# The second chunk of a fused attention and SwiGLU kernel: two orderings of the same work, and where float64 weights get their sign bits

## The chip, the cores and the metric

The kernel runs on one core of a Trainium2 chip. The metric is the device time of one execution in microseconds (us); lower is better. TensorE (PE) does the matmuls and PE transposes, VectorE (DVE) and ScalarE (ACT) the elementwise work, GpSimd (POOL) here only memsets and DMA issues, SyncE (SP) only DMA issues.

## The reference, cut to what matters

```
B, H, S, D = 4, 8, 768, 48;  d_model = H*D = 384;  d_ff = 1536
f = sigmoid(f_logit)                              # B,H,S,D
for t in range(S):                                # per batch and head
    state = f[:, :, t, :, None] * state + outer(k[:, :, t], v[:, :, t])
    y[:, :, t] = q[:, :, t] @ state
x   = y.transpose(0, 2, 1, 3).reshape(B * S, H * D)      # 3072 x 384
out = (silu(x @ w_gate) * (x @ w_val)) @ w_out           # weights arrive as float64
```

## The kernel before

**Units and chunks.** The sequence is cut into 6 chunks of 128 positions. A unit is one batch in one chunk; unit u is batch u % 4 of chunk u // 4. Each unit runs `attention(u)`, a generator that stops at some 15 places so that its steps can be set between other work. For a unit the kernel forms running products of the gates on DVE (two scans), multiplies k and q by them, takes the scores on PE (`sc`, L700), masks them on DVE (`A`, L719), multiplies by v on PE (`y`), and carries a state of 48x48 per head (`decayed`, `dS`, `state`). A chunk's four units make 512 tokens, which then go through the feed-forward part.

**Stages.** Stage 1 is the attention of chunk 0. Stage 2 is the feed-forward of chunk 0 by plain matmuls, with the attention of chunk 1 (units 4 to 7) set between them, and beside it the conversion of all weights. Stage 3 is the feed-forward of chunks 1 to 5 by products over sums of blocks (15 products in place of 18, 7 in place of 8), with the attention of the chunks after set between them. The change is in stage 2.

**Two ways to turn f, k and q.** A unit needs f, k and q with the head dimension on partitions. Plain units load rows and turn them by PE transposes against an identity (`fTp`, `kTp`, `qTp`, L614; 4 matmuls each), and turn k back the same way (`kt`, L704). Units for which `by_squares(u)` holds load the data already laid out in squares and turn them by DVE's 32x32 transposes (L630, L641, L685); k goes back through a DVE transpose (L668) and two DMAs over DRAM. In stage 2 of the kernel before units 5, 6 and 7 go by squares.

**Weights.** The float64 weights come in 18 pieces of 768 KB: six pairs of `w_gate` and `w_val`, two hidden blocks each, and six pieces of `w_out`. `fetch` issues the DMA on SP's queue into one of four buffers `w64`. `sizes` has ACT write the low mantissa part (`up`, L491) and the magnitude (`top`, L495). `join` has DVE clamp (L505), shift (L508 or L512) and add (L510, L516). The sign is the open matter: pieces listed in `SIGNED` (9 of the 18) get it from a third ACT instruction (L494); the others from a third DVE instruction that takes the two top bits out of `w64` (L514). `up` and `top` have two buffers each. The first pair is handled in halves, so that there are 20 joins.

**Feed-forward of chunk 0.** `mlp_plain(0)` gives 12 gate products and 12 val products (L836), each followed by a Silu on ACT or a multiplication on DVE, and 12 down steps (L859), each of four matmuls of 128x384, one for each of the four batches. PSUM has four banks for these (`m`) and four for attention (`a`).

**Sums of weights.** `weight_sums` gives 32 DVE additions over `w_both` into `extra` and back into `w_both`, which stage 3 needs; `token_sums` gives further ones over `xT`.

**Order of stage 2.** Each step of `mlp_plain` carries a planned duration (`PLAIN`, `PLAIN_DOWN`). Lists name the planned time at which each further step is issued: `JOINS_AT`, `SIZES_AT`, `FETCHES_AT`, `EARLY` for the four units and `SUMS_AT`. `in_turn_of_time` merges them:

```
for took, f in steps:
    come_in()                 # issue all that is due by now
    before = lagging[:]; lagging.clear()
    f()
    for g in before: g()      # Silu or multiplication, one step late
    now += took
```

After it `in_order` chains all of stage 2's instructions of PE, DVE, ACT and SP in that order.

Of the kernel before, what the change touches and what calls it, by code (L numbers as in the profile page):

```python
# [290 lines left out]
def short_path(ctx, tc, ident, least, judge, q, k, v, f_logit, moe_w_gate, moe_w_val, moe_w_out, out):  # L291
# [80 lines left out]
    middle = const.tile([128, 1], FP32, tag="middle", name="middle")  # L372
    nc.gpsimd.memset(middle, 32767.5)
# [29 lines left out]
    def by_squares(u):  # L403
        return u >= SQUARES * B - 3
# [26 lines left out]
    by_pool = []  # L431

# [26 lines left out]
    def weight_piece(dst, src, parts, signs):  # L459
# [27 lines left out]
        def sizes(m):  # L487
            lo, hi = halves(m)
            up = wst.tile(shape, I32, tag="up", name="up", bufs=NPART)
            ends = up.bitcast(U16).rearrange("p b a (n two) -> p b a n two", two=2)  # L490
            nc.scalar.activation(ends[:, :, :, :, 0], lo.bitcast(U32), AF.Copy, scale=2.0 ** -29)  # L491
            top = wst.tile(shape, I32, tag="top", name="top", bufs=NPART)
            if signs:
                nc.scalar.activation(ends.bitcast(mybir.dt.float16)[:, :, :, :, 1], high_ends(m), AF.Sign, bias=middle, scale=-1.0)  # L494
            nc.scalar.activation(top.bitcast(FP32), hi.bitcast(FP32), AF.Abs, scale=2.0 if signs else 1.0)  # L495
            kept["up", m], kept["top", m] = up, top

        def join(m, what=("clamp", "add")):
            lo, hi = halves(m)
            up, top = kept["up", m], kept["top", m]  # L500
            if "add" in what and "clamp" not in what:
                nc.vector.tensor_tensor(dst[:, part(m)].bitcast(I32), top, up, ALU.add)
                return
            step = 0x800000 if signs else 0
            nc.vector.tensor_scalar(top.bitcast(FP32), top.bitcast(FP32), as_float(0x38000000 + step), as_float(0x47F00000 + step),  # L505
                                    op0=ALU.max, op1=ALU.min)
            if signs:
                nc.vector.tensor_single_scalar(top, top, 3, op=ALU.logical_shift_left)  # L508
                if "add" in what:
                    nc.vector.tensor_tensor(dst[:, part(m)].bitcast(I32), top, up, ALU.add)  # L510
                return
            nc.vector.tensor_scalar(top, top, 3, 0x3FFFFFFF, op0=ALU.logical_shift_left, op1=ALU.bitwise_and)  # L512
            ends = up.bitcast(U16).rearrange("p b a (n two) -> p b a n two", two=2)
            nc.vector.tensor_single_scalar(ends[:, :, :, :, 1], high_ends(m), 0xC000, op=ALU.bitwise_and)  # L514
            if "add" in what:
                nc.vector.tensor_tensor(dst[:, part(m)].bitcast(I32), top, up, ALU.add)  # L516
# [15 lines left out]
    SIGNED = (4, 6, 7, 8, 9, 11, 15, 16, 17)  # L532

    def add_piece(dst, src, parts=1):
        fetch, *rest = weight_piece(dst, src, parts, len(fetches) in SIGNED)
        fetches.append(fetch)
        for group, fs in zip((sizes, joins), rest):
            group += fs
# [32 lines left out]
    owner = {}  # L571

    def owned(u, *names):
        assert all(owner[nm] == u for nm in names), (u, owner)

    def attention(u):
        b, c = units[u]
        rot = u % NROT if c < SQUARES else 0
# [16 lines left out]
        def decay():  # L595
            nonlocal diagonal
            if c:
                owner["decayed"] = u
                nc.vector.tensor_tensor(decayed[:, :, 0:D], states[b], whole.broadcast_to((128, HP, D)), ALU.mult)
# [28 lines left out]
        owner["gate", rot] = u  # L628
# [18 lines left out]
        owner["tail", rot] = owner["start"] = u  # L647
        owned(u, ("gate", rot))
# [12 lines left out]
        owned(u, ("tail", rot))  # L661
# [14 lines left out]
        if in_squares:  # L676

            (nc.scalar.copy if c >= SQUARES else nc.vector.tensor_copy)(least[:, u, :], whole.rearrange("p a t -> p (a t)"))
            whole = least[:, u, :].unsqueeze(2)
        owned(u, ("gate", rot), ("tail", rot), "start")  # L680
# [7 lines left out]
        owned(u, ("gate", rot), ("tail", rot))  # L688
        multiply(qT, qp, pairs(gate)[:, :, 1:N1])
        nc.gpsimd.memset(pairs(gate)[:, :, 0:1], 0.0)  # L690
# [37 lines left out]
        if c:  # L728
            owned(u, "decayed")
# [63 lines left out]
        if c == 0:  # L793
            nc.scalar.copy(states[b], dS)
        elif c < NCH - 1:
            owned(u, "decayed")
            nc.vector.tensor_tensor(states[b], decayed[:, :, 0:D], dS, ALU.add)
        yield

    def load_after(u, what):  # L800

        if u + 1 < len(units) and u + 1 != SQUARES * B:
            load(u + 1, what)

# [25 lines left out]
    def mlp_plain(c):  # L830
# [13 lines left out]
        def gate(j):  # L844
            p = product(w_gate, j, "gate")
            lag(nc.scalar.activation, part(j), p, AF.Silu)

        def val(j):
            p = product(w_val, j, "val")
            lag(nc.vector.tensor_tensor, part(j), part(j), p, ALU.mult)  # L850

        return [*[(PLAIN, lambda j=j, f=f: f(j)) for f, j in ((gate, 0), (val, 0), (gate, 1), (val, 1))],
                *[(PLAIN, lambda j=j, f=f: f(j)) for i in range(2, NF, 2) for f in (gate, val) for j in (i, i + 1)],
                *[(PLAIN_DOWN, f) for f in downs_abreast(c, h)]]
# [13 lines left out]
    def downs_abreast(c, h):  # L868
# [3 lines left out]
        def step(n):  # L872
# [3 lines left out]
            for b in range(B):  # L876
                down_part(banks[b], c, h, b, n)
                if n == NF - 1:
                    ob = rooms_of[b // 2][:, b % 2, :]
                    (nc.vector.tensor_copy if b % 2 else nc.scalar.copy)(ob, banks[b])  # L880
                    nc.gpsimd.dma_start(out=out[b * S + c * C:b * S + (c + 1) * C, :], in_=ob)
# [13 lines left out]
    PRODUCT, DOWN, PLAIN, PLAIN_DOWN = 0.86, 3.9, 2.57, 2.65  # L895
# [7 lines left out]
    def chain(k, q, qmul, turn=None, head=None):  # L903
# [10 lines left out]
        (chain(2.6, 4, 8.6), chain(14.5, 20, 23), chain(30, 37, 43.2), chain(57.4, 57.8, 61)),  # L914
# [12 lines left out]
    def score_bank(u):  # L927
# [6 lines left out]
    JOINS_AT = (0.8, 4.5, 5, 7.6, 13.2, 16.3, 20.3, 27.2, 29.6, 36.1, 38.7, 43.3, 46.6, 47.8, 55.3, 55.4, 67.6, 70.8)  # L934
    SIZES_AT = (0.39, 2.4, 6.2, 11.1, 13.2, 18.4, 18.6, 22.1, 31.8, 38, 39.8, 40.1, 43.1, 50.8, 53, 56, 64.8)
    FETCHES_AT = (-1.1, 0.6, 5.5, 5.9, 6, 9.2, 10.6, 21.1, 23.6, 27, 35.5, 35.5, 37.8, 42.4)
    EARLY = (
        (-1.01, 4.17, 4.58, 9.7, 9.87, 10.5, 11, 11.5, 12, 13.4, 17.3, 22, 28.4, 28.41, 33),
        (26, 31.3, 32.8, 34.3, 34.6, 34.6, 36.1, 37.4, 38.2, 40.6, 43.3, 43.4, 50.8, 54.81, 56),
        (46.2, 49.2, 50.7, 51.4, 51.5, 57, 57.6, 58, 62, 63.9, 64.4, 65.5, 68.2, 68.21, 70),  # L940
        (63, 64, 66.8, 66.9, 67.4, 67.9, 68.6, 71.6, 73.3, 75.9, 76, 76.7, 78, 78.41, 80.3))
    SUMS_AT = (64.3, 64.5, 72.58, 72.7, 74.06, 74.74, 75.3, 75.42, 75.98, 76.02, 76.18, 76.3, 76.66, 76.86,
        77.34, 77.54, 78.22, 78.5, 79.18, 79.86, 81.22, 81.26, 81.26, 81.34, 81.62, 81.9, 81.94, 82.58, 82.58, 82.7,
        83.2)
    LATE_SUMS_AT = (23,)
# [57 lines left out]
    def lag(f, *args):  # L1003
        lagging.append(lambda: f(*args))  # L1004
# [217 lines left out]
    def in_turn_of_time(waiting, steps):  # L1222

        waiting.sort(key=lambda x: x[0])
        now = 0.0

        def come_in():
            while waiting and waiting[0][0] <= now:
                waiting.pop(0)[1]()

        come_in()
        for took, f in steps:
            come_in()
            before = lagging[:]
            lagging.clear()
            f()
            for g in before:
                g()
            now += took
        come_in()  # L1240
        for g in lagging:
            g()
        lagging.clear()
        assert not waiting
# [41 lines left out]
    first_join(("clamp"))  # L1286
    sizes.pop(0)()
    run(B - 1, 3)
    first_join(("add"))
# [5 lines left out]

    waiting = [(t, sizes.pop(0)) for t in SIZES_AT]
    waiting += [(t, joins.pop(0)) for t in JOINS_AT]
    waiting += [(t, fetches.pop(0)) for t in FETCHES_AT]
    assert not fetches and not sizes and not joins
    waiting.append((-0.02, lambda: sigmoid_ahead(B)))  # L1300
    for b, at in enumerate(EARLY):
        run_of = attention(B + b)
        waiting += [(t, lambda run_of=run_of: next(run_of)) for t in at]
    sums_of = [weight_sums(odd) for odd in range(2)]
    sums = sums_of[0][0:7] + sums_of[1][0:7] + sums_of[0][7:] + sums_of[1][7:]
    waiting += zip(SUMS_AT, sums[:len(SUMS_AT)])
    in_turn_of_time(waiting, mlp_plain(0))
    in_order(mark, (mybir.EngineType.PE, mybir.EngineType.DVE, mybir.EngineType.Activation, mybir.EngineType.SP))

# [20 lines left out]

    assert len(SUMS_AT) + len(LATE_SUMS_AT) == len(sums)
    waiting += zip(LATE_SUMS_AT, sums[len(SUMS_AT):])
    waiting += [(at, f) for at, f in zip(DOWN_SUMS_AT, down_weight_sums())]
    blocks = {}

    def blocks_of(c):
        yield from blocks[c]
# [8 lines left out]
    in_turn_of_time(waiting, (step for c in range(1, NCH) for step in blocks_of(c)))  # L1346
# [78 lines left out]
```

## Time and profile before

| | |
|---|---|
| median of 3 runs | 597.66 us (597.51 to 597.72) |
| the profiled execution | 597.51 us, of which span 595.8 us and 1.71 us around it |
| stage 1, stage 2, stage 3 in the profile | 0 to about 30, 30 to 138.4, 138.4 to 595.8 us |
| PE, DVE, ACT, POOL busy over the span | 585.5, 479.3, 301.1, 112.8 us |
| granted TensorE clock | 1.000 |

Times are in us from the start of the span. In lists of instructions in order of time the first column is the start, the second the duration; where an engine waited, brackets give how long and for whom. Instructions of one engine overlap slightly, so that the distance from start to start is often a little under the duration. A matmul's end is modelled, so that a busy PE is not a PE at its peak.

### The profile page before, as it was taken

Reading aid. Unit: us, or ns where it says so; the run is one execution under the profiler, and the core shown is the slowest. Engines: PE = TensorE matmul, PEld = TensorE weight load, DVE = VectorE, ACT = ScalarE, POOL = GpSimd, SP = SyncE. Lnnn points to the kernel's source line nnn. Section 1 sums busy time; section 2 is a strip of 40 time slices with the busy share of each in tenths; the row PEclk is TensorE's granted clock in tenths of the full one; section 3 lists DMA queues with packets and bytes.
Section 4 is the critical chain, followed back from the end, with each engine's and each line's share of the span. In section 5 each row is a group of like instructions: output and inputs, shape, how many; then the busy total and the mean of one; then the engine's idle time right before and its main releaser. Section 6 shows DMA issues by size and latency. Waiting matters only on the chain.

```text
span 595.8 us, 10874 instructions
## 1 busy us (share of the span) xinstructions
PE 585.5 (98%) x3972; PEld 481.8 (81%) x3972; DVE 479.3 (80%) x830; ACT 301.1 (51%) x563; POOL 112.8 (19%) x240
## 2 busy tenths in 40 slices
PE   7899999999999999999999999999999999999996
PEld 4744444667888999888999888899988899988896
DVE  7997998999989877998986888994978972666741
ACT  3488677025877322676640667632476730356600
POOL 3140345202132330212030030330030330000000
PEclk9999999999999999999999999999999999999999
DMA  9999487233666565542345332543231100100001
GB/s 205 253 307 286 142 217 186 60 98 107 122 117 110 96 150 136 138 100 64 84 117 137 99 80 62 112 111 99 74 99 28 29 10 6 53 2 1 2 1 56
DMA packets 106291, 61.86 MB, mean 104 GB/s; under 512 B 64200, under 2 KB 97032, under 8 KB 106232
## 3 DMA queue, kind: packets, MB, share of 16 engines
q1 hardware_dynamic: 93800, 45.96, 31.0%
q0 software_dynamic: 10992, 13.19, 10.0%
q10 hardware_dynamic: 1440, 1.97, 0.9%
q8 instruction: 32, 0.52, 0.4%
q14 instruction: 27, 0.22, 0.1%
HBM read 47.64 MB, written 8.13 MB: 94 GB/s over the span
## 4 chain that ended last, share of the span: by engine, by line
PE 98%; DVE 1%; ACT 0%; issue 0%; DVEq 0%
PE o L1151 20%; PE A L1052 18%; PE B L1052 15%; PE c L1052 6%; PE o L1052 6%; PE o L859 5%; PE gate L836 5%; PE val L836 5%; PE sc L700 4%; PE o L1214 3%; PE y L746 3%; PE y L767 2%; PE dS L787 2%; PE y L742 2%; PE kt L704 1%; PE fTp L614 0%
## 5 line engine op out<-in xcount | busy, mean ns | idle before, releaser
L757 POOL DMA_DIRECT2D xT<-yT x120 | 59.8, 506 | 53.4 <-ACT yT L750 49.0
L1052 PE MATMUL A<-xs,w_both 128*128 128x256 f32 x240 | 62.2, 382 | 0.0
L1151 PE MATMUL o<-w_out,h 128*128 128x192 f32 x360 | 62.0, 327 | 0.0
L1151 PEld LDWEIGHTS o<-w_out,h 128*128 128x128 f32 x360 | 58.7, 190 | 1.0 <-issue 0.2
L1057 ACT COPY c<-A 128x512 f32<-128x512 f32 x40 | 23.3, 583 | 60.5 <-PE A L1052 59.4
L1057 ACT COPY aside<-A 128x512 f32<-128x512 f32 x60 | 35.2, 586 | 32.9 <-PE A L1052 32.7
L951 DVE TENSOR_TENSOR c<-c,aside 128x512 f32<-128x512 f32 x60 | 41.1, 685 | 12.8 <-ACT aside L1057 11.1
L1052 PEld LDWEIGHTS A<-xs,w_both 128*128 128x128 f32 x240 | 44.9, 190 | 6.6
L1004 DVE TENSOR_TENSOR h<-h,c 128x256 f32<-128x256 f32 x100 | 40.6, 414 | 7.6 <-ACT h L1068 7.3
L954 DVE TENSOR_TENSOR c<-c,aside 128x512 f32<-128x512 f32 x60 | 41.0, 684 | 2.7 <-ACT aside L1057 2.7
L1068 ACT ACTIVATE h<-c 128x256 f32<-128x256 f32 x100 | 39.4, 417 | 5.0 <-DVE c L951 3.8
L719 DVE TENSOR_TENSOR A<-sc,causal 128x512 f32<-128x512 f32 x48 | 30.9, 685 | 13.4 <-PE sc L700 13.4
L1151 PE MATMUL o<-ws,h 128*128 128x192 f32 x240 | 41.5, 328 | 0.0
L1052 PE MATMUL B<-xs,w_both 128*128 128x256 f32 x160 | 41.3, 380 | 0.0
L1052 PE MATMUL A<-xs,extra 128*128 128x256 f32 x160 | 41.2, 380 | 0.0
L1052 PE MATMUL c<-xT,w_both 128*128 128x256 f32 x160 | 41.1, 379 | 0.0
L1052 PE MATMUL B<-xT,extra 128*128 128x256 f32 x160 | 41.0, 379 | 0.0
L1057 ACT COPY aside<-B 128x512 f32<-128x512 f32 x60 | 35.2, 586 | 9.0 <-PE B L1052 7.0
L1151 PEld LDWEIGHTS o<-ws,h 128*128 128x128 f32 x240 | 39.1, 190 | 0.5
L954 DVE TENSOR_TENSOR c<-o,c 128x512 f32<-128x512 f32 x40 | 27.4, 686 | 11.0 <-ACT h L1068 6.2
L951 DVE TENSOR_TENSOR c<-c,o 128x384 f32<-128x384 f32 x15 | 8.2, 548 | 34.8 <-PE o L1151 34.8
L690 POOL MEMSET gates<- 128x4 f32 x24 | 3.6, 150 | 169.0 <-DVE qT L593 163.9
(163 smaller groups left out, 1240.2 us busy)
## 6 DMA issues: line engine op xcount, KB each, us to landing
fsquares<-in_f_logit_dram SPq DMA_DIRECT2D x64, 96.0 KB, 4.1
qsquares<-in_q_dram SPq DMA_DIRECT2D x64, 96.0 KB, 2.3
ksquares<-in_k_dram SPq DMA_DIRECT2D x64, 96.0 KB, 2.4
w<-in_moe_w_gate_dram SPq DMA_DIRECT2D x6, 768.0 KB
w<-in_moe_w_val_dram SPq DMA_DIRECT2D x6, 768.0 KB, 6.5
w<-in_moe_w_out_dram SPq DMA_DIRECT2D x6, 768.0 KB, 8.8
v<-in_v_dram SPq DMA_DIRECT2D x19, 192.0 KB, 2.8
turn<-ksquares SPq DMA_DIRECT2D x40, 64.0 KB, 2.2
```

The lines of the kernel that those rows point to most:

```text
L700: nc.tensor.matmul(sc[par][:, a * C:(a + 1) * C], lhsT=kT[r, a, :], rhs=qT[r, a, :], start=True, stop=True)
L719: nc.vector.tensor_tensor(A[:, par], sc[par].rearrange("p (a t) -> p a t", t=C), causal.unsqueeze(1).broadcast_to((128, HP, C)), ALU.mult)
L757: (nc.gpsimd if c >= SQUARES else nc.sync).dma_start(out=xT[c][f % 128:f % 128 + n, f // 128, b * C:(b + 1) * C], in_=yT[r:r + n, par, a / ...
L836: nc.tensor.matmul(p, lhsT=w[:, j, i, :], rhs=xT[c][:, i, :], start=(i == 0), stop=(i == KT - 1))
L859: nc.tensor.matmul(p, lhsT=hidden_tile(h, n // 2)[:, n % 2 * 2 + b // 2, b % 2 * C:(b % 2 + 1) * C], rhs=w_out[:, j, :], start=(n == 0), s ...
L951: nc.vector.tensor_tensor(dst, a, b, ALU.add)
L954: nc.vector.tensor_tensor(dst, a, b, ALU.subtract)
L1004: lagging.append(lambda: f(*args))
L1052: nc.tensor.matmul(p[name][:, n, :], lhsT=weights_of[a][:, n, j, :], rhs=tokens[b], start=fresh and n == 0, stop=True, skip_group_check=True)
L1057: nc.scalar.copy(t, p[name])
L1068: nc.scalar.activation(dst, src[:, 0, :], AF.Silu)
L1151: nc.tensor.matmul(p[:, n, :], lhsT=lhsTs[j][:, n * C:(n + 1) * C], rhs=rhs[:, j, :], start=first and j == order[0] and n == 0, stop=j == ...
```

## The change

The changed kernel orders stage 2 in another way, and three pieces of work go to other engines with it.

1. The lists of times are gone. The first steps of stage 2 are written out one by one and chained by `in_order`; the rest is made by `take_turns`, which hands out the steps of units 4 to 7 evenly among the feed-forward steps, with one `weights()` (one fetch, one size, one join) after each pair of products and four more among the down steps, and the sums woven into the down steps. This rest is not chained: the scheduler of the language places it.
2. `SIGNED` is gone: all 18 pieces get their sign on DVE. ACT's third instruction goes away nine times; DVE's third one comes nine times.
3. `by_squares` starts at unit 6 in place of unit 5: unit 5 loads rows through SP's queue and is turned on PE.
4. The Silu and the multiplication follow their product at once and no longer lag a step; the four output DMAs of chunk 0 go from GpSimd's queue to ACT's; the copy of `least` for units 6 and 7 goes from DVE to ACT; all 32 sums lie ahead of stage 3's lists (one had been in stage 3).

Stage 1 and the order of PE in stage 3 are as before.

```
-        return u >= SQUARES * B - 3
+        return u >= SQUARES * B - 2
...
-            if signs:
-                nc.scalar.activation(ends...[:, :, :, :, 1], high_ends(m), AF.Sign, bias=middle, scale=-1.0)
-            nc.scalar.activation(top.bitcast(FP32), hi.bitcast(FP32), AF.Abs, scale=2.0 if signs else 1.0)
+            nc.scalar.activation(top.bitcast(FP32), hi.bitcast(FP32), AF.Abs)
...
-    SIGNED = (4, 6, 7, 8, 9, 11, 15, 16, 17)
...
-                    nc.gpsimd.dma_start(out=out[b * S + c * C:b * S + (c + 1) * C, :], in_=ob)
+                    nc.scalar.dma_start(out=out[b * S + c * C:b * S + (c + 1) * C, :], in_=ob)
...
+    def attention_steps(c):
+        runs = [attention(c * B + b) for b in range(B)]
+        order = sorted((2 * b + s, b, n) for b in range(B)
+                       for s, n in enumerate((1, 8, 3, 3) if by_squares(c * B + b) else (3, 6, 3, 3)))
+        return [lambda b=b, n=n: [next(runs[b]) for _ in range(n)] for _, b, n in order]
...
+    def take_turns(first, second, rest):
+        done = 0
+        n = len(first) - rest
+        for i, f in enumerate(first):
+            f()
+            want = min(i + 1, n) * len(second) // n
+            for g in second[done:want]:
+                g()
+            done = want
...
-    in_turn_of_time(waiting, mlp_plain(0))
-    in_order(mark, (mybir.EngineType.PE, mybir.EngineType.DVE, mybir.EngineType.Activation, mybir.EngineType.SP))
+    hidden, last = mlp_plain(0)
+    steps = attention_steps(1)
+    sigmoid_ahead(B)
...
+    weights()
+    load(B + 1)
+    hidden[2]()
+    steps.pop(0)()
+    in_order(mark, (mybir.EngineType.PE, mybir.EngineType.DVE, mybir.EngineType.Activation, mybir.EngineType.SP))
+    hidden = [f for i in range(NF) for f in hidden[2 * i:2 * i + 2] + [weights]][4:]
+    del hidden[1]
+    for i in range(len(joins) - hidden.count(weights)):
+        last.insert(3 * i, weights)
...
+    take_turns(hidden + weave(last, sums_of[0][3:7] + sums_of[1][3:7] + sums_of[0][7:] + sums_of[1][7:]), steps, 8)
```

## The prediction

> **What bounds the kernel now.** I read the table by stage first, then the list of PE's waits, then PE and DVE in order of time around the places where the order changes. The table gives for each stretch the busy time of PE, PEld, DVE, ACT and POOL with their counts, the granted clock, the DMA share and GB/s; the first row is stage 2, the second stage 3.
>
> ```profile
> 30.00:138.40 108.40, 108.40 (x532) 57.32 (x531) 98.59 (x165) 63.20 (x85) 31.93 (x60) 1.00 0.66 177
> 138.40:595.80 457.40, 452.60 (x3106) 405.91 (x3104) 354.16 (x623) 225.81 (x453) 73.49 (x151) 1.00 0.33 78
> ```
>
> PE is busy for all 108.40 us of stage 2 and 452.60 of 457.40 us of stage 3, at the full clock; the list of PE's waits holds nothing between 30 and 138 us. So the change can win only by taking work off PE in stage 2 or by packing it tighter, and it loses by each instruction that it puts on PE and each wait that it causes there. DVE (98.59 of 108.40) is close behind; ACT has 45 us to spare. The next views are PE and DVE in order of time (start, duration, engine, line, tile; in brackets the wait before it).
>
> ```profile
> 39.92 0.60 PE L614 MATMUL kTp<-idf,kraw 128*128 128x128 f32 x4
> 40.36 0.60 PE L614 MATMUL qTp<-idf,qraw 128*128 128x128 f32 x4
> 40.80 5.32 PE L836 MATMUL gate<-xT,w_both 128*128 128x512 f32 x12
> 46.04 1.16 PE L700 MATMUL sc<-qT,kT 48*128 48x128 f32 x16
> 47.13 0.66 PE L704 MATMUL kt<-idf,kT 128*128 128x128 f32 x4
> 47.62 0.59 PE L836 MATMUL val<-xT,w_both 128*128 128x512 f32 x1
> ```
>
> A group of four transposes takes 0.44 us from start to start (39.92 to 40.36, 40.36 to 40.80), or 0.49 for `kt` (47.13 to 47.62). Unit 4's scores start at 46.04 as soon as PE is free.
>
> ```profile
> 37.63 0.56 DVE L505 TENSOR_SCALAR top<-top 128x768 f32<-128x768 f32 x1 [0.34 <-ACT top L495]
> 38.70 0.60 DVE L514 TENSOR_SCALAR up<-w 128x768 uint16<-128x768 uint16 x1
> 39.34 0.96 DVE L516 CUSTOM_DVE_ANT_0 w_both<-top,up 128x1536 uint16<-128x1536 uint16 x1
> 44.07 0.69 DVE L593 TENSOR_TENSOR qT<-qTp,gates 128x512 f32<-128x512 f32 x1
> 44.95 0.62 DVE L505 TENSOR_SCALAR top<-top 128x768 f32<-128x768 f32 x1
> 47.07 0.55 DVE L505 TENSOR_SCALAR top<-top 128x768 f32<-128x768 f32 x1
> 49.65 0.68 DVE L719 TENSOR_TENSOR A<-sc,causal 128x512 f32<-128x512 f32 x1
> ```
>
> `qT`, which those scores need, is done at 44.07 + 0.69 = 44.76, 1.28 us before PE takes it. That is the slack to be used up. The join at 44.95 has its sign from ACT and ends where the next starts: 47.07 − 44.95 = 2.12 us. The one at 47.07 takes its sign on DVE: 49.65 − 47.07 = 2.58 us.
>
> **Unit 5 goes from squares to PE transposes.** PE gets `fTp`, `kTp`, `qTp` and `kt`, 16 matmuls: 3 × 0.44 + 0.49 = 1.81 us. PE never waits in stage 2, so this cannot fall into a gap: **+1.8 us**, the surest term. DVE loses unit 5's four square transposes (f 0.98, k 0.61, k back 0.63, q 0.72 from start to start), 2.9 us, and the small copies of `least`. The loads of unit 5 go through SP as rows and are issued long before they are used; nothing on PE waits for loads here: 0.
>
> **The sign of nine more pieces on DVE.** 9 × (2.58 − 2.12) = 4.1 us onto DVE; ACT is relieved of nine of L494, 1.15 each, 10.3 us. With the transposes gone DVE grows by some 1.2 us net and would stand near 100 of 108.4 + 1.8. As a sum this has cover; what counts is where DVE comes late for something that PE needs. By the Trainium skill, "Perfetto Trace Analysis", section "Optimizing Scalar/DVE Operations", work is given to ScalarE where VectorE is saturated; this change does the reverse. Read as if DVE were the bound, that would put all 4.1 us into the time (603.6 in place of 599.5 for the transposes alone); the row of stage 2 has PE full and DVE with 9.8 us idle.
>
> **Unit 4's scores, the first place where DVE comes late.** In the changed order DVE does not take the fourth piece's clamp after the first multiplication `h`. It first takes the top bits of the *fifth* piece out of `w` (L505 in the new numbering, the old L514), which waits for that piece's DMA; then the rest of the fourth piece, the tails' scan, the fifth piece's clamp, `kT`, the gates' scan, `h`, and `qT`. Queued behind this one wait are thus all of unit 4's products, and PE's scores wait for them. When does the fifth piece land? (SP and ACT in order of time, and a row of the page's list of DMA issues, whose last column is the time from issue to landing.)
>
> ```profile
> 31.50 0.37 SPq L474 DMA_DIRECT2D w<-in_moe_w_gate_dram  x1
> 39.15 1.08 ACT L491 ACTIVATE up<-w 128x768 uint16<-128x768 uint32 x1 [1.01 <-DMA w<-in_moe_w_gate_dram]
> w<-in_moe_w_out_dram SPq DMA_DIRECT2D x6, 768.0 KB, 8.8
> ```
>
> Issued at 31.50, it released ACT at 39.15, 7.65 us later. The pieces of `w_gate` lie between 5.9 and 11.5 us with median 6.5, those of `w_out` at 8.8. The issue is at about the same place in SP's queue in both kernels, so I take 39.15 again. Then: 39.15 + 0.51 (the bits, start to start) + 7.13 (the row at 37.63 up to the end of `qT` at 44.76, same instructions less one bit step and plus one) + 0.4 (the fifth piece's clamp, set between) − 0.2 (the fourth piece's clamp no longer waits for its `top`) = about 47.0. PE gets to the scores at 46.04, or 46.1 since unit 4's `fTp` only changes places with a product. **+0.9, taken as 1.0 us** with one crossing between engines. If the piece lands 1.2 us earlier (6.5) it is 0; at 8.8 us it is 2.2, at 11.5 it is 4.9. "DMA: Bandwidth & Descriptors", section "Anatomy of one DMA — SWDGE (gpsimd) path", gives about 2.0 us plus bytes over 436e3 per us, an estimate of 3.8 us for 768 KB. The wait would be nothing by it and the sum 599.6; but it is written for GpSimd's queue, and no piece in this trace landed under 5.9 us.
>
> **Unit 5's scores.** From unit 4's scores to unit 5's PE needs 75.74 − 46.04 = 29.70 us in the kernel before, and 3 × 0.44 more in the one after (`kt` comes behind): 31.0 us. DVE has 51 instructions in that stretch of the new order: 17 clamps, shifts and scalings of 0.56, 7 joins of 0.96, 7 bit steps of 0.60, 4 scans of 1.22, 10 multiplications of 0.68, a transpose of 1.11 and small ones: 34.6 us of durations. They overlap: between 60.77 and 98.54 us 59 instructions with durations of 40.2 us took 37.8, 0.042 each, and independent neighbours reach 0.085. So 30.3 to 32.4 us, a wait of 0 to 1.4. The seven joins lie back to back with other pieces' steps, so mostly independent: **+0.2 us**.
>
> **w_out's joins and the down steps.** In the new order the joins of the fourth, fifth and sixth piece of `w_out` each wait for a down step of PE to release the room, and a later down step waits for the join. By the same walk there are 0.9, 2.2 and 1.1 us of slack: **0**, with 0 to 3.9 as bounds (three times a join of 0.96 and a crossing of some 0.3).
>
> **What costs nothing.** The Silu and the multiplication follow their product at once rather than one step late: ACT has 45 us to spare, and a product of 5.3 us hides 0.60 + 0.69. The four output DMAs of chunk 0 on ACT's queue: 0.87 us per pair of issues there, ahead of copies that PE takes much later; if that cover went, 2 × 0.87. The copy of `least` is 0.19 on ACT. One sum out of stage 3 (0.68 on DVE, which has 103 us idle there), and stage 3's PE order stays: 0. Nothing that PE waits for moves over POOL's queue.
>
> **Sum.** 597.51 (profiled execution: 595.8 of span and 1.71 around it) + 1.8 + 1.0 + 0.2 = 600.5. The median stands 0.15 over that execution: **600.7**. About 0.2%, 1.2 us, can be told from no change here.
>
> **Rivals and chances.**
> *The walk as above*, each wait within some tenths: 600.0 to 601.6. Chance 0.45.
> *Transposes only*: the fifth piece lands by 38.0, or DVE's start-to-start overlap is at its best, and no wait is left: 597.66 + 1.8 = 599.5 (599.2 to 599.9). For it: half of the `w_gate` pieces land within 6.5 us; against: 7.65 in this very place. Chance 0.2.
> *The fifth piece lands late* (8.8 to 11.5 us, as `w_out` and the slowest `w_gate` did, with unit 5's row loads now on the same queue): a wait of 2.2 to 4.9, that is 601.9 to 604.6. Chance 0.15.
> *DVE falls behind PE in the down steps*: the three joins' loop closes, each with 1.3 us: 600.7 + 3.9 = 604.6, more if DVE is behind by the whole 4.1 us from unit 5 on. For it: DVE at 91% before; against: slacks of 1 to 2 us. Chance 0.13.
> *Not slower*: PE's "busy" hides waits. Five blocks of 12 matmuls behind attention's small matmuls take 5.35 us, others 5.15. If that 5 × 0.2 is idleness between groups that the new, looser order removes, and the piece lands early, 597.66 + 1.8 − 1.0 = 598.5, within the 1.2 us. It decides once the gains from packing pass 0.6 us with no wait at unit 4. No row shows PE stopped, so 0.07.
>
> **How the numbers follow.** The likeliest case gives 600.7. The range runs from transposes only (599.2) to a piece that lands at the latest that the rows show (604.6); outside are "not slower" and half of the DVE case with its excess. Faster by over 0.2% would need packing gains of 3 us beyond anything in the rows: 0.02. Within 0.2%: the rest of "not slower", 0.05. Slower: 0.93.
>
> **What would show it.** Right: 16 more 128x128 transposes in stage 2 with unit 5's at some 0.44 us a group; DVE waiting for a DMA at the bit step near 37 to 39 us; PE waiting for DVE's `qT` about 1.0 us near 46 to 47 us, and for little else; stage 3 starting near 141.4 in place of 138.44 and lasting as long as before. Wrong: waits of PE at a down step or at later scores (DVE behind in general), a fifth piece that lands before 38 us, a stage 3 whose length changes, or stage 2 no longer than before in spite of the 16 transposes.

## The result, and the profile after

The changed kernel takes 599.34 us (median of 14 runs, 599.19 to 599.66) against 597.49 us for the kernel before: 1.85 us more, ratio 1.0031 (95% interval 1.0022 to 1.0039). The profiled execution took 599.19 us, its span 597.5 us against 595.8 us. The prediction was 600.7 us, range 599.2 to 604.6, a growth of 3.0 us over its 597.66 us; the direction held and the time lies at the low end of the range, where the rival "transposes only" had 599.5 us.

The table by stage of the changed kernel (columns as before: PE, PEld, DVE, ACT, POOL busy with counts, clock, DMA share, GB/s), cut where stage 3 now starts:

```profile
30.00:139.93 109.93, 109.93 (x552) 59.23 (x551) 99.55 (x171) 57.55 (x81) 22.77 (x42) 1.00 0.54 165
139.93:597.50 457.57, 452.69 (x3106) 405.97 (x3104) 352.08 (x618) 226.18 (x453) 71.87 (x148) 1.00 0.32 78
```

PE is again busy for the whole of stage 2; stage 3 is as long as before within 0.2 us. The list of PE's waits holds nothing in stage 2. So stage 2's growth, 139.93 − 138.44 = 1.49 us, is work and not waiting. PE in order of time shows which:

```profile
46.16 1.16 PE L681 MATMUL sc<-qT,kT 48*128 48x128 f32 x16
...
55.47 0.60 PE L599 MATMUL fTp<-idf,fraw 128*128 128x128 f32 x4
55.91 2.74 PE L821 MATMUL gate<-xT,w_both 128*128 128x512 f32 x6
...
71.06 0.60 PE L599 MATMUL kTp<-idf,kraw 128*128 128x128 f32 x4
71.50 0.60 PE L599 MATMUL qTp<-idf,qraw 128*128 128x128 f32 x4
71.93 5.32 PE L821 MATMUL val<-xT,w_both 128*128 128x512 f32 x12
77.18 1.16 PE L681 MATMUL sc<-qT,kT 48*128 48x128 f32 x16
78.27 0.66 PE L685 MATMUL kt<-idf,kT 128*128 128x128 f32 x4
78.76 5.32 PE L821 MATMUL gate<-xT,w_both 128*128 128x512 f32 x12
```

Unit 5's four groups take 0.44, 0.44, 0.43 and 0.49 us from start to start: 1.80 us. Unit 4's scores start at 46.16, 0.12 later than before, with no wait. Of the sum 0.12 + 1.80 = 1.92 us, 1.49 are left at stage 3. The rest, 0.43, went back at three places: the gate block behind unit 5's scores starts at 78.76 and the next block at 83.92, 5.16 later, where before it came right behind the scores and took 5.26; unit 5's `dS` now stands next to its `y` and not between two blocks of products (0.25); and the last val block comes behind a gate block in place of behind that `dS` (96.48 to 101.64 is 5.16 us, 5.26 before).

Why unit 4's scores did not wait, in DVE's and SP's order of time, and GpSimd's in the kernel before:

```profile
37.17 0.61 DVE L505 TENSOR_SCALAR up<-w 128x768 uint16<-128x768 uint16 x1
...
44.71 0.69 DVE L579 TENSOR_TENSOR qT<-qTp,gates 128x512 f32<-128x512 f32 x1
```

```profile
31.51 0.37 SPq L473 DMA_DIRECT2D w<-in_moe_w_gate_dram  x1
31.97 0.43 SPq L456 DMA_DIRECT2D fraw<-in_f_logit_dram  x1
...
37.08 0.70 SPq L473 DMA_DIRECT2D w<-in_moe_w_val_dram  x1
```

```profile
31.61 2.23 POOL L449 DMA_DIRECT2D fraw<-in_f_logit_dram  x4 [1.22 <-ACT fraw L568]
```

The bit step of the fifth piece (37.17) has no bracket: the piece had landed at most 37.17 − 31.51 = 5.66 us after its issue, where it took 7.65 us before. When it landed before that, no row says. `qT` was done at 45.40, 0.76 before PE wanted it.

### The profile page after: what moved, and what is told of

The parts are those of the page before. It is cut to its first block, busy times and chain, and to the rows that moved or that the text cites. A ratio compares the mean times of both kernels' runs of the same rounds, so it can differ in the third digit from the quotient of the medians.

```text
span 597.5 us, 10878 instructions
## 1 busy us (share of the span) xinstructions
PE 587.1 (98%) x3988; PEld 484.3 (81%) x3988; DVE 478.2 (80%) x832; ACT 295.8 (50%) x560; POOL 101.1 (17%) x217
## 3 DMA queue, kind: packets, MB, share of 16 engines
q0 software_dynamic: 9696, 10.50, 7.5%
## 4 chain that ended last, share of the span: by engine, by line
PE 98%; DVE 1%; ACT 0%; issue 0%; DVEq 0%; ACTq 0%
PE o L1124 20%; PE A L1025 18%; PE B L1025 14%; PE c L1025 6%; PE o L1025 6%; PE o L844 5%; PE gate L821 5%; PE val L821 5%; PE sc L681 4%; PE o L1187 3%; PE y L725 3%; PE y L746 2%; PE dS L766 2%; PE y L721 1%; PE kt L685 1%; PE fTp L599 0%
```

## The experiments

In some executions PE's first transposes run slower (unit 0's `kTp` 1.08 us in place of 0.75 in number 1), or a load of stage 1 lands later, which moves all that follows by up to 1.4 us. So beside the times I compare a stretch that holds stage 2 alone: from the start of the last `dS` of stage 1 to the first A product of stage 3, in the profiled executions. In the kernel before it is 138.44 − 28.52 = 109.92 us, in the changed one 139.93 − 28.52 = 111.41. What a run loses in stage 1 or stage 3 is not in it. The medians stand beside 597.5 to 597.7 us for the kernel before, timed together with each; a ratio is to that. "New" order includes item 4 of the change, which no run separates from it.

| order | signs of the nine | unit 5 | stretch, over before | median us | ratio, 95% |
|---|---|---|---|---|---|
| old | ACT | PE | +1.71 | 600.37 | 1.0033 to 1.0061 |
| old | DVE | squares | +1.91 | 599.24 | 1.0016 to 1.0040 |
| old | DVE | PE | +3.07 | 601.16 | 1.0044 to 1.0070 |
| new | ACT | squares | +1.26 | 598.85 | 1.0011 to 1.0034 |
| new | ACT | PE | +3.84 | 601.43 | 1.0049 to 1.0075 |
| new | DVE | squares | +2.86 | 602.09 | 1.0070 to 1.0098 |
| new | DVE | PE (the changed kernel) | +1.49 | 599.34 | 1.0022 to 1.0039 |

**1. The kernel before with unit 5 on PE.**

```
-        return u >= SQUARES * B - 3
+        return u >= SQUARES * B - 2
+    waiting.append((-0.5, lambda: load(B + 1)))
```

> The kernel before with this one part of the change: unit 5 loads rows through SP's queue and is turned on PE. Theory (the transposes are the loss): 597.5 + 4 groups of 0.44 to 0.49, less up to 0.35 for blocks that now follow each other more closely: 598.9 to 599.4, and no wait of PE in stage 2. Rival (the loss comes from the order and the signs): 597.5.

PE has no wait in stage 2, and the stretch is 1.71 us longer: the 16 transposes alone, as the theory had it. The median is 1.0 us above the upper end of what was expected. The profiled execution, at 601.29 us, had the slow start (stage 2 begins 1.35 us later) and a stage 3 that is 0.6 us longer; whether the other four had the same is not shown (the lowest took 599.75).

**2. The kernel before with all signs on DVE.** Edit: `SIGNED = ()`.

> The kernel before with the list of pieces signed on ACT made empty, so that nine more pieces get their sign from DVE; nothing else is changed. Theory (DVE has cover, only lateness towards PE counts): 597.3 to 598.0, with 4.1 us more DVE busy time in stage 2 and no wait of PE above some tenths. Rival (DVE is near enough to its limit to pass it on): up to 4.1 us more, 601.6, with PE waiting for DVE at scores or at down steps.

The theory missed. PE in order of time:

```profile
109.90 1.09 PE L746 MATMUL y<-A,v 128*64 128x128 f32 x16
112.69 0.67 PE L787 MATMUL dS<-v,kt 128*64 128x48 f32 x16 [1.69 <-DMA kt<-turn]
```

And DVE and GpSimd:

```profile
97.52 0.70 DVE L668 STREAM_TRANSPOSE kraw<-kT 128x512 f32<-128x512 f32 x1
107.17 0.71 POOL L715 DMA_DIRECT2D kt<-turn  x1
```

DVE turned unit 6's k back at 97.52 in place of 95.37, GpSimd issued `kt` at 107.17 in place of 103.98, and PE stood for 1.69 us. DVE's idle time lay elsewhere than its lateness.

**3. The changed kernel with unit 5 back in squares.** Edit: the bound 3 again, without `load(B + 1)`.

> The changed kernel with unit 5 put back to squares (the bound of by_squares is 3 units again, the row load of unit 5 left out); order, signs on DVE and all else as changed. Theory (the 16 PE transposes are the whole loss): the 1.85 us go, less a few tenths of packing that the new order gains: 597.2 to 597.6, stage 3 near 138.2 us. Rival (the loss is in the order and the signs): it stays near 599.3. Second part of the theory: the fifth weight piece landed early in the changed kernel because unit 5's row loads held the sixth piece back on SP's queue and unit 5's square loads were gone from GpSimd's; with both back it lands near 39 us again, DVE waits about 1.5 us at the fifth piece's bit step, and PE about 0.9 us at unit 4's scores: then 598.1 to 598.6.

Both parts of the theory fell. It is the slowest of all; in stage 2 DVE and behind it ACT come late:

```profile
93.57 2.84 PE L821 MATMUL gate<-xT,w_both 128*128 128x512 f32 x6 [1.22 <-ACT h L831]
104.18 1.56 PE L844 MATMUL o<-w_out,h 128*128 128x384 f32 x4 [1.02 <-DVE h L835]
```

Outside the stretch this execution lost 1.3 us more behind PE's last matmul (6.1 us from its end to the end of the span, in place of 4.8), for a cause that stays open.

And the fifth piece still landed within 5.75 us, although the sixth was issued at 33.24 again. What differs from the kernel before is that the square loads of f on GpSimd's queue came at 33.08 and not at 31.61, right behind the piece's issue at 31.50. With that issue 0.1 us behind its own the piece took 7.65 us (the kernel before), 8.44 (number 2), 9.28 (number 11) and 10.50 (number 7, the first of its two), but at most 6.53 in number 10. In the nine other executions, where these loads come 1.6 us later or unit 5's rows come on SP's queue in their place, it never took more than 6.54. So these loads are a likely cause, not an isolated one.

**4. The new order alone**: unit 5 by squares and the nine signs on ACT (L494 and `SIGNED` put back).

> The changed kernel with both transfers of work undone: unit 5 by squares again and the nine pieces signed by ACT's third instruction again; the new order, the unlagged Silu and multiplication and the output DMAs on ACT's queue remain. It shows what the order alone does. Theory (the order costs nothing by itself; unit 5's squares and nine signs on DVE together were too much for DVE in the run before): no wait of PE for ACT's Silu or DVE's multiplication between 85 and 110 us, and 0.25 to 0.35 us gained because attention's groups follow each other: 597.1 to 597.6. Rival (the looser order itself makes DVE late): 599 to 602.

The rival was nearer: PE waits 0.77 us for ACT's Silu at 90.35 and 0.37 for DVE at 102.58. The new order by itself, with item 4, costs 1.26 us.

**5. The changed kernel with the signs on ACT.**

> The changed kernel with the nine signs back on ACT, unit 5 still turned on PE. Theory (with unit 5 off DVE the signs are fully covered there): DVE busy some 4 us less in stage 2, and the time unchanged: 599.0 to 599.6. Rival (the signs cost in this order what they cost in the old one, 1.7 us): 597.6.

Neither. Taking work off DVE made it 2.1 us slower. ACT in order of time, and PE behind it:

```profile
101.72 0.20 ACT L671 COPY least<-tails 128x4 f32<-128x4 f32 x1 [2.41 <-DVE tails L645]
101.93 1.28 ACT L843 ACT_TABLE_LOAD   x1
103.23 1.08 ACT L843 ACTIVATE h<-gate 128x512 f32<-128x512 f32 x2
```

```profile
103.88 2.85 PE L856 MATMUL o<-w_out,h 128*128 128x384 f32 x8 [1.81 <-ACT h L843]
```

The Silu stands behind a table load, that behind the copy of `least`, and that waits for DVE's scan of the tails, which came 3.5 us later than in the changed kernel (101.72 against 98.24). The new order's rest is not chained, and each edit there came out with another order of DVE and ACT. Numbers 3 to 5 are therefore each a schedule of its own, and their differences are no clean prices.

**6. The old order with both transfers of work** (edits 1 and 2 together).

> The kernel before with both transfers of work and its own order: nine more signs on DVE and unit 5 turned on PE. Theory (PE's transposes also free DVE of some 3 us, which takes away the wait for unit 6's k that the signs caused alone): from the first gate product to stage 3 110.5 us as with the transposes alone, whole time 599.3 to 599.9 where the start is as in the kernel before. Rival (the two costs add): 112.2 us and 601.3.

Rather the rival: +3.07 where the two add to 3.62; the wait for `kt` is 1.14 us. So in stage 2 the new order is worth 3.07 − 1.49 = 1.6 us to this share of work, and costs 1.26 us with the old share.

**7. Unit 6's turn of k earlier**, once in number 2 and once in number 6, in the list of times:

```
-        (46.2, 49.2, 50.7, 51.4, 51.5, 57, 57.6, ...
+        (46.2, 49.2, 50.7, 51.4, 51.5, 55.2, 57.6, ...
```

> The kernel before with all nine signs on DVE (as in the run with the empty list) and one DVE instruction moved: unit 6's turn of k back (L668) stands right behind its kT, ahead of two joins in place of behind them. Theory (the signs cost only by way of unit 6's k, which was turned late and whose trip over DRAM then held up dS by 1.69 us): the turn comes some 5 us earlier, the wait at dS is gone, stage 3 starts at 138.5 to 138.8 in place of 140.38, and the time is 597.6 to 598.3. Rival (DVE is simply too full): another wait takes its place, 599.2.

> The old order with both transfers of work, nine signs on DVE and unit 5 on PE, and the same single move of unit 6's turn. Theory (in the changed kernel the new order's gain is that unit 6's k goes back earlier): the wait of 1.14 us at unit 6's dS is gone, what is left over the kernel before is the 16 transposes, 1.7 us: 599.2 to 600.0, the changed kernel's time. Rival (the new order helps in other ways): about 601.2 as without the move.

The wait at `dS` is gone in both; the stretches are +0.14 and +2.02. Number 2 fell to 598.54 us (interval 1.0003 to 1.0021), a little above the theory's 598.3; number 6 stayed at 601.14 (1.0041 to 1.0069), as its rival had it. So the late turn was the cost of the signs in stage 2, and not their whole cost. A new wait took over at the third product of stage 3, 0.47 us in the first and 0.56 in the second. DVE and PE of the first of the two:

```profile
139.24 0.68 DVE L951 TENSOR_TENSOR w_both<-w_both 128x512 f32<-128x512 f32 x1
...
140.64 0.54 DVE L880 COPY ob<-o 128x384 f32<-128x384 f32 x1
```

```profile
141.28 1.10 PE L1052 MATMUL o<-xT,w_both 128*128 128x256 f32 x4 [0.47 <-issue]
```

The product starts 0.1 us after the second `ob` copy ends (141.18), which stands behind all sums of weights in DVE's queue; in the kernel before that copy ended at 139.96 and the product followed at 140.17 without a wait. The profile names "issue", so that the copy held it is read from the times only. In the changed kernel DVE waits for PE at the same place, and two sums come behind the copies:

```profile
140.13 0.56 DVE L865 COPY ob<-o 128x384 f32<-128x384 f32 x1 [0.73 <-PE o L844]
140.60 0.68 DVE L924 TENSOR_TENSOR w_both<-w_both 128x512 f32<-128x512 f32 x1
```

**8. The fifth piece later in the changed kernel**: `load(B + 1)` ahead of `weights()`.

> The changed kernel with one exchange on SP's queue: unit 5's four row loads are issued ahead of the fifth weight piece in place of behind it. The piece is then issued near 36.8 us in place of 31.5 and should land near 42.4 in place of before 37.2. Theory (the walk of unit 4's scores): DVE waits at the fifth piece's bit step until then, qT is done near 50.6 in place of 45.4, PE waits about 4.4 us at unit 4's scores, and the whole time grows by as much: near 603.7. Rival (later slack in the order takes it up, or the scores do not hang on it): 599.3 to 600.5.

The rows were issued earlier than I had assumed (27.36), so that the piece went out at 32.36 and landed by 38.69:

```profile
38.69 0.61 DVE L505 TENSOR_SCALAR up<-w 128x768 uint16<-128x768 uint16 x1 [1.44 <-DMA w<-in_moe_w_gate_dram]
...
45.75 0.68 DVE L579 TENSOR_TENSOR qT<-qTp,gates 128x512 f32<-128x512 f32 x1
```

```profile
46.58 1.16 PE L681 MATMUL sc<-qT,kT 48*128 48x128 f32 x16 [0.36 <-DVE qT L579]
```

The size was wrong and the mechanism right: DVE waits, `qT` ends at 46.43, PE waits 0.36, and stage 3 starts 0.41 later. The prediction's walk with 38.69 in place of 39.15 gives 38.69 + 0.51 + 7.13 + 0.4 − 0.2 = 46.53. The median, 600.70 us (1.0047 to 1.0087), spreads from 599.74 to 603.36, and only the fastest of these was profiled.

**9. Unit 6 on PE as well.** Edit: the bound 1, with `load(B + 2)`.

> The changed kernel with one more unit by rows: unit 6 too is loaded through SP's queue and turned on PE, 16 transposes more. Theory (PE has no gap in stage 2, each unit turned on PE adds four groups of 0.44 to 0.49 us): 1.5 to 1.8 us more than the changed kernel, 600.8 to 601.2. Rival (DVE's relief gives something back or other waits go): under 600.3.

601.69 us, 2.35 more than the changed kernel and above what the theory had; the stretch grows by 2.25. Its four groups are 0.44, 0.43, 0.44 and 0.50 us; unit 6's `y` was cut in two by a down step, which adds 0.36 us for the two products ahead of it. No wait of PE in stage 2. The four groups put 1.8 us on PE in each case; with what the order around them does, a unit turned on PE cost 1.71 (number 1) to 2.25 us.

**10. Three signs only**, those of `w_out`'s last pieces: `SIGNED = (4, 6, 7, 8, 9, 11)`.

> The kernel before with only the last three of the nine pieces (the ones of w_out) signed on DVE in place of ACT. Theory (signs cost only where they make DVE late for something with a long tail, and that was unit 6's k, which goes back over DRAM: DVE turned it 2.15 us later and its kt was issued 3.2 us later, with 1.5 us of slack at dS): of these three only one join lies ahead of that place, so kt is some 0.5 us later, nothing waits, and the time is 597.4 to 597.8. Rival (each sign on DVE costs its share, 1.9 us over nine): 598.1.

598.35 us (1.0006 to 1.0024), above both figures. As the theory said, nothing waits at unit 6's `dS` and the stretch is +0.17; but the third product of stage 3 is late as in number 7 (0.34 us of "issue", 0.58 in all): DVE's lateness reached PE at another place.

**11. Packing in the kernel before**: unit 5's `y` right ahead of its `dS` (50.8 becomes 54.8 in its list of times).

> The kernel before with one step moved in its list of times: unit 5's y products come 4 us of planned time later, right ahead of its dS, so that the gate product between them goes ahead of both. Theory (a block of wide matmuls next to attention's small ones is about 0.1 us longer, and each break between groups costs it again; that is where the changed kernel's 16 transposes got 0.3 us back): stage 3 starts 0.3 to 0.35 us earlier, at 138.1 in place of 138.44, and the time is 597.1 to 597.3, at the edge of what the timed runs resolve. Rival (the rows of busy PE hold no such price): 138.4 and 597.5. It would be a version faster than both.

```profile
82.73 5.31 PE L836 MATMUL val<-xT,w_both 128*128 128x512 f32 x12
87.88 5.31 PE L836 MATMUL gate<-xT,w_both 128*128 128x512 f32 x12
93.12 0.67 PE L742 MATMUL y<-qT,decayed 48*64 48x128 f32 x16
...
94.64 0.62 PE L787 MATMUL dS<-v,kt 128*64 128x48 f32 x16
```

The val block in front takes 5.15 us (82.73 to 87.88) in place of 5.24, and the stretch is 109.58 us, 0.34 less with the same instructions. The median is 597.34 against 597.67 us, ratio 0.9992 with an interval of 0.9983 to 1.0001: the shift is plain in the trace, and as a gain in time just not settled. It is the only version here below both kernels.

## Why the prediction was right or wrong

The number lies in the range because a rival came true that had a chance of 0.2, and not the course with 0.45. Of the 1.2 us of waits in the sum none came, and the prediction's own sign of being wrong, a fifth piece that lands before 38 us, did. What it had right is the mechanism of the main term: PE has no gap, so the transposes cost their full time. In the profiled executions the growth of 1.68 us is 1.80 of transposes, 0.12 at the start of stage 2, where unit 4's `fTp` now stands between two products, 0.43 given back by packing, and 0.19 in stage 3.

*The transposes, +1.8.* Right: 1.80 in the changed kernel, 1.71 net alone (number 1), 1.81 again for unit 6 (number 9).

*Unit 4's scores, +1.0.* This step failed, and in one term: "so I take 39.15 again". The piece landed by 37.17. The walk that starts from it held to 0.1 us in number 8. I had put the issue at the same place and not asked what else was in flight, though the change itself takes unit 5's loads off GpSimd's queue (number 3 tells how far that goes). The figures beside it were misread too: 5.9, 6.5 and 11.5 us are the least, the median and the most of the `w_val` and `w_out` pieces, since the profile gives no landing for `w_gate`; so they were no odds for this piece. The 3.8 us of "DMA: Bandwidth & Descriptors" of the Trainium skill (section "Anatomy of one DMA — SWDGE (gpsimd) path") led to the right sum, no wait, but no run shows that time for this piece: where a wait gives its landing it took 6.33 (number 8) to 10.50 us, and 5.66 in the changed kernel is only an upper bound.

*Unit 5's scores, +0.2, and the down steps, 0.* The list of waits has neither: 0 and 0.

*Signs on DVE as covered.* Right for this kernel: no wait of PE in stage 2. But the ground given was thin. The prediction weighed 4.1 us against 9.8 us of idle time, said that lateness is what counts, and then walked only the scores and the down steps. It wrote that nothing PE waits for moves over POOL's queue; unit 6's `kt` does, and in the old order the same signs cost 1.91 us by that one trip (number 2). In the changed kernel it leaves far earlier, long before `dS` at 114.86:

```profile
87.13 0.70 DVE L649 STREAM_TRANSPOSE kraw<-kT 128x512 f32<-128x512 f32 x1
96.96 0.71 POOL L696 DMA_DIRECT2D kt<-turn  x1
```

It also puts sums behind the `ob` copies. That these two things are the cover is argued: no run makes the turn late in the new order. The Trainium skill's advice to give work to ScalarE where VectorE is saturated ("Perfetto Trace Analysis", "Optimizing Scalar/DVE Operations") would, if DVE at 91% is taken as saturated, have asked for the reverse of this change; number 2 agrees with it and number 5 does not, since there PE waits for ACT's Silu, itself held up behind DVE's late scan.

*"What costs nothing".* The Silu, the copies and the DMAs on ACT cost PE nothing in the changed kernel. It is no property of these edits: with the old share of work the order costs 1.26 us (number 4).

*Not slower, by packing.* Its mechanism exists (number 11 shows it alone) and was at work: 0.43 us of PE's "busy" came back. It was sized at 1.0 and treated as a rival, where it belonged into the sum: 597.49 + 1.8 − 0.4 = 598.9; the rest of the way to 599.34 is the 0.12 and 0.19 above, and some 0.15 that the medians differ by more than the profiled executions. Its rows were misread as well: of the ten blocks of 12 in the kernel before one takes 5.35 us from start to start, seven 5.24 to 5.26 and two 5.15 or 5.16, which is 0.9 over 5.15 in all.

*Stage 3, 0.* Mostly right: its length grew by 0.2. One product near the end is 0.3 us late:

```profile
564.36 1.13 PE L1025 MATMUL A<-xT,w_both 128*128 128x256 f32 x4 [0.17 <-ACT aside L1030]
```

The same 0.3 us stands in numbers 1 and 8 and in none of the other kernels. The instructions around it are the same in all. Its cause stays open.

## What to carry to other kernels

Where the bounding engine has no gap, price a change by the instructions that it puts on that engine and by what each break between unlike groups of its work costs; that sum, worked out afterwards, came to within 0.5 us here. Cover for another engine is not its idle share but the slack at each instruction that the bound waits for: the same nine signs cost 1.9 us of stage 2 in the old order, because one turn of k with a long trip behind it came 2 us late (0.14 with that turn moved ahead), and no wait shows in the changed kernel. And a transfer's time should not be carried from one kernel to the other where the change also moves the loads around it.

## What the runs showed of the hardware that was not expected

Blocks of 12 wide matmuls (128x512) take 5.15 us from start to start next to each other and 0.1 more on either side of attention's small ones, without any wait in the profile; placing groups together gave 0.34 us (number 11). The same piece of 768 KB took from at most 5.66 to 10.50 us to land. And the first transposes of an execution may run slower, by up to 1.4 us in all. The traces' records of the granted clock begin with full clock at 11.27 us in number 1 and at 5.40 us in the kernel before, and six bf16 matmuls take 2.77 us from 8.49 in the one and 1.46 from 7.59 in the other; what was granted before the first record is not shown. "TensorE: Matmul & The Clock Gate" of the Trainium skill (Part 1, the HAM clock gate) says that how long the array stays at its lower clock at the start differs from run to run, which would fit.
